# The second product of the last layer by Strassen's scheme, in pairs of column tiles

## The chip, the cores and the metric

One core of a Trainium2 chip runs the whole program in one launch. The metric is the device time of that launch in microseconds (us), from the median of several executions. TensorE (PE) multiplies, VectorE (DVE) and ScalarE (ACT) split operands and evict sums, GpSimd (POOL) helps in some stages, and SyncE's queue (SP) issues most transfers.

## The reference, cut to what matters

Four layers work on x of 2048 x 640: a spectral filter, a token-mixing MLP, and both again. The last layer is the second MLP. S = 2048 tokens, D = 640 channels, F = 1728 hidden units:

```python
def _B_ref(x, w1, b1, w2, b2):
    h = _layernorm(x, axis=-1)                   # (B, S, D)
    u = jnp.einsum("bsd,sf->bdf", h, w1) + b1    # (B, D, F)
    u = _gelu(u)
    y = jnp.einsum("bdf,fs->bds", u, w2) + b2    # (B, D, S)
    return y.transpose(0, 2, 1)
x = x + _B_ref(_layernorm(x, axis=-1), B_w1, B_b1, B_w2, B_b2)
```

All is float32 at the inputs and outputs.

## The kernel before, in words

Each float32 operand is split into two float16 parts, a high one (`wh`, `hh`, `uh`) and a low one (`wl`, `hl`, `ul`); a product is three matmuls, high x high, high x low and low x high (`mm3`). A matmul has 128 rows of contraction, 128 output partitions and 320 of the 640 columns, so a tile of results takes two banks of PSUM, one per half `a`; `big()` gives out such two-bank tiles, four in all.

`b` is the MLP; it is called with `li` = 1 and `li` = 3, and `last` is true for the second. Its first product makes 14 tiles of 128 hidden units (the 14th has 64, held twice), each over 16 tiles of tokens: 16 x 6 matmuls a tile, 64 for the 14th. For the first two tiles PE does the products with the high parts first (`high`) and those with the low parts `hl` of the input behind them (`rest`), since `hl` is made meanwhile on DVE. A tile's sums go through bias and GELU (names `t` and `q`) and are split into `uh[ft]` and `ul[ft]`.

The second product makes 16 column tiles j, each over the 14 tiles of hidden units and two halves: 13 x 2 x 3 matmuls, and 2 x 2 for the last tile, of which one of each two has 64 rows (`wl[:64, ft]`). `wsplit` makes a tile's `wh` on ACT and `wl` on DVE from the raw weights, one tile ahead; `wload` issues the loads on SP's queue three tiles ahead. The bias goes onto the residual `xt` on ACT, and one DVE instruction a tile adds the scaled sums to it, in two halves for the last tile, where PE takes half 0 first. Then `xt` is stored.

A scheduler orders the instructions of each engine where code isn't pinned (`self.pin`); the start of `b` is pinned, the rest of it isn't.

Of the kernel before, what the change touches and what calls it, by code (L numbers as in the profile page):

```python
# [53 lines left out]
class Layers:  # L54
# [41 lines left out]
    def setup(self):  # L96
        nc, A = self.nc, self.A
        base = self.base = self.push("base", side="left")
        self.psum = self.push("ps", bufs=4, space=PSUM)
        self.dram = self.push("dr", space=DRAM)  # L100
        self.mh = base.tile([128, 1], F32, name="mh")
        nc.vector.memset(self.mh, -0.5)
        self.eps = base.tile([128, 1], F32, name="eps")
        nc.vector.memset(self.eps, EPS)
        self.b1 = base.tile([128, NFT], F32, name="b1s")
        self.b2 = base.tile([128, NJ], F32, name="b2s")
        self.junk = base.tile([128, 8, 128], BF16, name="junk")
# [5 lines left out]
        self.qt = base.tile([128, NFT], F32, name="qt")  # L113
        self.su, self.iu = (base.tile([128, 1], F32, name=a) for a in ("su", "iu"))
# [690 lines left out]
    def wtile(self, m):  # L805

        return (0, m, NJ) if m < NFT else (1, m - NFT, NFT)

    def wload(self, m):
        k, t, n = self.wtile(m)  # L810
        src = self.A["w2" if k else "w1"][t]
        raws = self.wraws[m] = []
        for c in (0, n // 2):
            raws.append(self.t(self.wr[max(m - 2, 0) % 3], [128, 8, 128], F32, "raw", 2)[:, :n // 2])
            self.nc.sync.dma_start(raws[-1], src[:, c:c + n // 2])
# [5 lines left out]
    def wsplit(self, m, cs=(0, 1), hi=True, lo=True, part=slice(None)):  # L821

        V, T, (k, t, n) = self.V, self.T, self.wtile(m)
        sc = self.st[k][:, t:t + 1]
        (wh, wl), raws = self.w[m], self.wraws[m]
        for c in cs:
            raw, a = raws[c][:, part], slice(c * n // 2, c * n // 2 + n // 2)
            h, l = wh[:, a][:, part], wl[:, a][:, part]
            if m == NFT - 1:

                T.activation(h[:, :, :64], raw[:, :, :64], AF.Identity, scale=sc)
                T.activation(l[:, :, 64:], raw[:, :, 64:], AF.Identity, scale=sc)
                V.scalar_tensor_tensor(
                    h[:, :, 64:], raw[:, :, 64:], sc, l[:, :, 64:], op0=ALU.mult, op1=ALU.subtract
                )
# [7 lines left out]
    def b(self, li):  # L843
        nc, A = self.nc, self.A
        V, G, T = self.V, self.G, self.T
        mm = self.PE.matmul
        first, last = li == 1, li == 3
        ph = self.push("h", side=self.sq)
# [11 lines left out]
        self.pop("hf")  # L860
        self.wr[1:] = (self.push(a, side=self.sp) for a in ("wr", "wr2"))
# [3 lines left out]
        if first:  # L865
            pf = self.push("uf", side=self.sp)
            uf = [pf.tile([128, 2, 320], F32, name=f"uf{f}_{self.n}") for f in range(NFT)]
            sc = {m: self.scale1(m) for m in range(2, NFT + NJ)}
        p = self.push("b1", side=self.sq)
# [16 lines left out]
        def step(m):  # L886
            if first and m in sc:
                next(sc[m])

        def usplit(ft, t):  # L890
            if first:
                V.tensor_scalar(uh[ft], t, self.su, None, op0=ALU.mult)
            else:
                T.activation(uh[ft], t, AF.Identity, scale=self.su)
            c = slice(0 if ft < NFT - 1 else 64, 128)
# [35 lines left out]
        for j in high(1, pss[1], w[1]):  # L931
            if first and j in (8, 10):
                self.scan1(2, (j // 2 - 4,))
            if j == 15:
                step(2)
        for ft in range(NFT):
# [9 lines left out]
            for j in run:  # L946
# [3 lines left out]
                elif ft == 1:  # L950
                    if j in (1, 2):
                        next(steps)
                    if first and j in (8, 10):
                        self.scan1(3, (j // 2 - 4,))
                    if j == 15:
                        step(3)
                else:
                    if ft == 2 and j in (4, 5):
                        step(3)
                    if first and ft == 2 and j in (5, 6):  # L960
                        self.scan1(4, (j - 5,))
# [4 lines left out]
                    if ft == 2 and j in (10, 11) or ft > 2 and j in (4, 5):  # L966
                        step(ft + 2)
                    if first and j == 8 and ft == NFT - 3:
                        self.scale_u()
                    if first and j in (11, 13):  # L970
# [3 lines left out]
                    if first and ft == NFT - 1 and 6 <= j:  # L974
                        usplit(j - 6, uf[j - 6])
# [14 lines left out]
            T.activation(q, q, AF.Tanh, scale=GS * GC)  # L990
            if first:
                V.scalar_tensor_tensor(uf[ft], q, 1.0, t, op0=ALU.add, op1=ALU.mult)
            else:
                V.scalar_tensor_tensor(t, q, 1.0, t, op0=ALU.add, op1=ALU.mult)
                usplit(ft, t)
        if first:
            for k in range(10, NFT):
                usplit(k, uf[k])
            self.pop("uf")
# [4 lines left out]
        if not last:  # L1004
            self.a0_open()
            for q in range(4):
                self.a0_load_m(q)
            self.a0_load()
        else:
            self.pT = self.push("a0", side=self.sp)  # L1010
        p = self.pT
# [13 lines left out]
        for j in range(NJ):  # L1025
# [10 lines left out]
            order = [(ft, a) for ft in range(NFT) for a in range(2)]  # L1036
            if last and j == NJ - 1:
                order.sort(key=lambda q: q[1])
            for i, (ft, a) in enumerate(order):
                if i in (4, 8):  # L1040
                    next(steps, None)
                if i in (6, 7):
                    step(m + 2)
                if first and i in (15, 18):
                    self.scan1(m + 3, (i // 3 - 5,))
# [8 lines left out]
            x2 = xt.rearrange("p (a b) -> p a b", a=2)  # L1054
            if last and j == NJ - 1:
                for a in range(2):
                    V.scalar_tensor_tensor(x2[:, a], ps[:, a, :320], c2, x2[:, a], op0=ALU.mult, op1=ALU.add)
                    nc.sync.dma_start(self.xs[li + 1][j][:, a * 320:a * 320 + 320], x2[:, a])
                continue
            V.scalar_tensor_tensor(x2, ps[:, :, :320], c2, x2, op0=ALU.mult, op1=ALU.add)  # L1060
            nc.sync.dma_start(self.xs[li + 1][j], xt)
            if last:
                continue
            if j == NJ - 1:
# [11 lines left out]
        self.pop("wb")  # L1076

    def run(self):
        nc, A = self.nc, self.A
        self.setup()  # L1080
        self.wa = self.push("wa", side="left")
        self.wp, self.wr = [self.wa, None], [self.push("wraw", side="left"), None, None]
        self.w, self.wraws = {}, {}
# [242 lines left out]
def _layout(inp):  # L1326
# [7 lines left out]
    a["w1"] = g("B_w1").reshape(128, 16, 1728)[:, :, fi].reshape(128, 16, 14, 128).transpose(2, 0, 1, 3)  # L1334
    a["w2"] = g("B_w2")[fi].reshape(14, 128, 128, 16).transpose(3, 1, 0, 2)
    a["b1"] = g("B_b1")[fi].reshape(14, 128).T
    a["b2"] = g("B_b2").reshape(128, 16)
# [26 lines left out]
```

## Time and profile before

| | us |
|---|---|
| median of 3 runs | 1085.15 (1084.61 to 1086.13) |
| the profiled execution | 1084.86 |
| its span, first to last instruction | 1083.1 |
| last layer, first product, to PE's change of product | 723.4 to 894.05 |
| last layer, second product | 894.05 to 1078.95 |
| last instruction behind PE's end | some 4.1 |

| engine | busy in the span | share |
|---|---|---|
| PE | 1030.8 us | 95% |
| DVE | 643.6 us | 59% |
| ACT | 553.9 us | 51% |
| POOL | 289.4 us | 27% |

The rows are from one profiled execution. Times count from the first instruction. "PE busy" counts a matmul from its start to its modelled end, and since matmuls overlap, the distance between starts is what one costs in a stream.

### The profile page before, as it was taken

The numbers are of one execution on the slowest core, as the hardware profiler recorded it, in microseconds if no ns is written. First come the engines' busy times: TensorE is split into PE (matmuls) and PEld (weight loads), VectorE is DVE, ScalarE is ACT, GpSimd is POOL, SyncE is SP. The second block draws the span as 40 slices with busy tenths as digits, with TensorE's granted clock in tenths as the row PEclk, the third lists the DMA queues.
The fourth block names the chain that finished last, engine by engine and source line by source line (L and its number), as shares of the span: only waits on it lengthen the run. The fifth ranks groups of instructions, "written<-read, shape, count | busy, mean of one in ns | idle before, by whom it ended". The sixth has DMA issues, their size and how long they took to land.

```text
span 1083.1 us, 21299 instructions
## 1 busy us (share of the span) xinstructions
PE 1030.8 (95%) x8515; PEld 777.2 (72%) x8515; DVE 643.6 (59%) x1311; ACT 553.9 (51%) x860; POOL 289.4 (27%) x491
## 2 busy tenths in 40 slices
PE   4889798999999999999997998999999999999998
PEld 3768698777777767777776878877777776666665
DVE  7979879954335856566746995995343334223221
ACT  5857768675445555555432775864433344222220
POOL 6938877200000002211221886840000000000000
PEclk8599999999999999999998998999999999999999
DMA  7766255523222264444224633644222233433411
GB/s 234 255 192 193 80 195 184 185 89 104 82 79 68 69 240 134 138 126 130 84 76 129 207 97 130 212 146 156 83 91 81 81 106 113 161 118 133 158 51 37
DMA packets 55738, 141.48 MB, mean 131 GB/s; under 512 B 6460, under 2 KB 12248, under 8 KB 55384
## 3 DMA queue, kind: packets, MB, share of 16 engines
q1 hardware_dynamic: 54200, 131.97, 37.5%
q0 software_dynamic: 1440, 8.15, 2.4%
q8 instruction: 67, 1.10, 0.4%
q14 instruction: 31, 0.25, 0.1%
HBM read 117.03 MB, written 23.07 MB: 129 GB/s over the span
## 4 chain that ended last, share of the span: by engine, by line
PE 76%; DVE 16%; POOL 2%; issue 2%; ACT 1%; DMA 1%; SPq 0%; DVEq 0%; ACTq 0%; POOLq 0%
PE ps L46 76%; DVE xt L46 5%; DVE st L46 2%; DVE el L46 2%; DVE f L46 2%; DVE s1l L46 1%; DVE hl L46 1%; DVE ta L46 1%; DVE xl L46 1%; DMA xt<-x 1%; POOL eo L46 0%; POOL ta L46 0%; DMA rest<-s1l 0%; DVE tb L46 0%; DVE mv L46 0%
## 5 line engine op out<-in xcount | busy, mean ns | idle before, releaser
L46 PEld LDWEIGHTS <-wh 128*128 128x128 f16 x3520 | 340.0, 98 | 138.3 <-issue 1.8
L46 PE MATMUL ps<-uh,wl 128*128 128x320 f16 (+1 forms) x896 | 268.4, 300 | 0.0
L46 PE MATMUL ps<-ul,wh 128*128 128x320 f16 x896 | 267.3, 299 | 0.0
L46 PE MATMUL ps<-uh,wh 128*128 128x320 f16 x832 | 248.9, 299 | 0.0
L46 PEld LDWEIGHTS <-wl 128*128 128x128 f16 x1728 | 168.7, 98 | 76.6 <-issue 8.7
L46 DVE SCALAR_TENSOR_TENSOR wl<-raw,s,wh 128x896 f16<-128x896 f32 (+2 forms) x120 | 139.2, 1173 | 112.9 <-ACT wh L46 112.6
L46 PE MATMUL ps<-hh,wh 128*128 128x320 f16 x896 | 194.8, 299 | 1.4 <-ACT hh L46 1.4
L46 ACT ACTIVATE wh<-raw,s 128x896 f16<-128x896 f32 (+2 forms) x124 | 126.6, 1044 | 131.0 <-PE ps L46 130.3
L46 PE MATMUL ps<-hl,wh 128*128 128x320 f16 x896 | 184.8, 299 | 0.0
L46 PE MATMUL ps<-hh,wl 128*128 128x320 f16 x832 | 181.1, 299 | 0.0
L46 POOL TENSOR_TENSOR r<-v,mh 128x1 f32<-128x1 f32 x64 | 35.8, 559 | 340.8 <-DVE nm L46 325.3
L46 DVE SCALAR_TENSOR_TENSOR xt<-ps,c,xt 128x640 f32<-128x640 f32 (+1 forms) x33 | 28.4, 863 | 139.6 <-PE ps L46 135.9
L46 ACT ACTIVATE junk<-raw 128x896 bf16<-128x896 f32 (+1 forms) x60 | 59.6, 993 | 48.5 <-DMA raw<-w 48.3
L46 ACT ACTIVATE xt<-xt,b2s 128x640 f32<-128x640 f32 x32 | 26.3, 821 | 91.1 <-DMA xt<-x 90.9
L46 DVE TENSOR_TENSOR f<-eo 128x256 f32<-128x256 f32 (+1 forms) x128 | 40.1, 366 | 41.8 <-POOL eo L46 41.2
L46 PE MATMUL ps<-tDi,yh 128*128 128x322 f32 x256 | 61.1, 326 | 2.6 <-ACT yh L46 1.7
L46 DVE BATCH_NORM_STATS2 st<-xt 128x6 f32<-128x320 f32 x128 | 56.2, 481 | 5.1 <-DMA xt<-x 4.9
L46 POOL TENSOR_TENSOR eo<-z 128x320 f32<-128x320 f32 x63 | 54.2, 881 | 17.0 <-ACT z L46 15.1
L46 PE MATMUL ps<-ph,tS 128*128 128x321 f16 (+2 forms) x288 | 57.9, 286 | 0.0
L46 PE MATMUL ps<-tM,f 128*128 128x128 f32 x160 | 38.3, 409 | 20.4 <-DMA xt<-x 11.9
L46 ACT ACTIVATE z<-xt,nb,r 128x640 f32<-128x640 f32 x31 | 28.5, 919 | 54.1 <-POOL z L46 43.6
L46 PEld LDWEIGHTS ps<-tM,f 128*128 128x128 f32 x160 | 32.3, 290 | 26.2 <-DVE f L46 25.7
(142 smaller groups left out, 1678.9 us busy)
## 6 DMA issues: line engine op xcount, KB each, us to landing
raw<-w SPq DMA_DIRECT2D x56, 512.0 KB
raw<-w SPq DMA_DIRECT2D x64, 448.0 KB
xt<-x SPq DMA_DIRECT2D x80, 320.0 KB
w<-w SPq DMA_DIRECT2D x48, 321.0 KB
x<-xt SPq DMA_DIRECT2D x48, 320.0 KB
out<-xt SPq DMA_DIRECT2D x15, 320.0 KB
tIM<-tIM POOLq DMA_DIRECT2D x8, 512.0 KB, 4.7
tDi<-tDi POOLq DMA_DIRECT2D x2, 1932.0 KB, 9.9
```

What stands on the lines that cost most here:

```text
L46: i = f(*a, **k)
```

## The change

The last layer has its own function now, `b2nd`; `b1st` is the old `b` without its branches for the last layer. In `b2nd` the second product takes column tiles d and d + 8 together, d = 0 to 7. The 14 tiles of hidden units are seen as seven in an upper half and seven in a lower half; the two halves of columns are 320 each. So a pair is a product of 2 x 2 quarters, A11, A12, A21, A22 of the weights by B11, B12, B21, B22 of the hidden units. Strassen's scheme (Winograd's form) makes it from seven products of quarters: A11 B11, S1 T1, S2 T2, S3 T3, A12 B21, S4 B22, A22 T4. The S are sums and differences of weight quarters (128 x 896, formed on DVE by `form`), the T are differences of quarters of the hidden units (`usums`, on DVE in the first product). Each product is seven tiles of contraction by one `mm3`, 21 matmuls of 128 rows. The lower half's 14th tile is filled with zeros in a copy of the weights (`w2z`).

The first product takes its tiles in the order `SEQ`: 6, 13, then 0, 7, 1, 8 and so on, so that tiles t and t + 7 stand together and tile 13, the one with 64 units, is the second. The hidden units are kept as seven quarters per t, high and low.

In the second product the loop over n = 0 to 55 is pinned on all engines. At step n PE gets product n, then the eviction of product n - 1 is issued, the high split of product n + 3 (ACT), the low split of n + 2 (DVE), and the forming of an operand four or five products ahead. Products 0 to 3 are arranged so that products 2 and 3 leave out the tile that was made last (`LATE`) and take it at the end. A11 and S1 of a pair lie in one two-bank tile, S2 and S3 in another, A12 takes the bank of A11, S4 and A22 take the banks of S2 and S3. A product is added to as many quarters of the result as need it. Weights are loaded four tiles ahead. The scale `US` is halved.

```diff
+NQ = 8
+SEQ = [6, 13] + [t + 7 * i for t in range(6) for i in range(2)]
...
     def wtile(self, m):
-        return (0, m, NJ) if m < NFT else (1, m - NFT, NFT)
+        k, i = m // NFT, m % NFT if m < NFT else m - NFT
+        if self.second:
+            i = i // 2 + i % 2 * NQ if k else SEQ[i]
+        return min(k, 1), i, NFT if k else NJ
...
+        u = [pu.tile([128, 2, 7, 320], F16, name=f"u{f}_{self.n}") for f in range(7)]
...
+        PQ = ("A11", "B11"), ("S1", "T1"), ("S2", "T2"), ("S3", "T3"), ("A12", "B21"), ("S4", "B22"), ("A22", "T4")
...
+        def form(n):
...
+            x, y, op = {
+                "S1": ((d, "A21"), (d, "A22"), ADD), "S2": (n - 1, (d, "A11"), SUB),
+                "S3": ((d, "A11"), (d, "A21"), SUB), "S4": ((d, "A12"), n - 3, SUB),
+            }[a]
+            x, y = (src[q] if isinstance(q, int) else raw(*q) for q in (x, y))
+            V.tensor_tensor(s, x, y, op=op)
...
+        def high(m, ps, w):
+            for j in range(NJ):
+                prod(ps, w[0], j, self.h[j][0], start=j == 0)
+                if not dup(m):
+                    prod(ps, w[1], j, self.h[j][0])
...
+        BK = {"A11": (0, 0), "S1": (0, 1), "S2": (1, 0), "S3": (1, 1), "A12": (0, 0), "S4": (1, 0), "A22": (1, 1)}
...
+        def evict(n):
...
+            if a == "A11":
+                part["m1"] = self.t(p, [128, 320], F32, "m1", 2)
+                T.activation(part["m1"], ps, AF.Identity, scale=c)
+                add(x[:, 0, 0], x[:, 0, 0])
+            if a == "S1":
+                add(x[:, :, 1], x[:, :, 1], both2(ps))
+            if a == "S2":
+                part["u2"] = self.t(p, [128, 320], F32, "u2", 2)
+                add(part["u2"], part["m1"])
+                V.tensor_tensor(x[:, 0, 1], x[:, 0, 1], part["u2"], op=ADD)
+            if a == "S3":
+                u3 = self.t(p, [128, 320], F32, "u3", 2)
+                add(u3, part["u2"])
+                V.tensor_tensor(x[:, 1], x[:, 1], both2(u3), op=ADD)
...
+            if a == "A12":
+                add(x[:, 0, 0], x[:, 0, 0])
+            if a == "S4":
+                add(x[:, 0, 1], x[:, 0, 1])
+                nc.sync.dma_start(out[d], row(d, 0))
+            if a == "A22":
+                add(x[:, 1, 0], x[:, 1, 0])
...
+        FORM = {3: 5, 5: 4, 6: 4, 1: 4}
+        for n in range(NP + 1):
+            d, i = n // 7, n % 7
+            if i == 0 and n < NP:
+                bank[d] = self.big(), self.big()
...
+            late = n in (2, 3)
+            if n < NP:
+                js = [j for j in range(7) if j != LATE]
+                product(n, js if late else js + [LATE], not late)
+            if n == 3:
+                for k in (2, 3):
+                    product(k, [LATE])
+            for k in {0: (), 3: (), 4: (2, 3)}.get(n, (n - 1,)):
+                evict(k)
+            if n:
+                hi(n + 3)
+            if n > 1:
+                lo(n + 2)
+            if i in FORM:
+                form(n + FORM[i])
```

At the start of the last layer DVE has, before the change, the last statistic `nb`, the two low splits of the second weight tile, and the low halves `hl`:

```order
L46 TENSOR_SCALAR nm_10281<-mv_10277 128x1
L46 TENSOR_TENSOR nb_10285<-nm_10281,r_10283 128x1
L46 SCALAR_TENSOR_TENSOR wl_9597<-raw_9592,s_72,wh_9596 128x1024
L46 SCALAR_TENSOR_TENSOR wl_9597<-raw_9594,s_72,wh_9596 128x1024
L46 TENSOR_TENSOR hl_1492_10312<-hf_1275_9372,hh_1118_7816 128x640
L46 TENSOR_TENSOR hl_1492_10314<-hf_1275_9373,hh_1118_7817 128x640
```

And DVE at the same place after the change:

```order
L48 TENSOR_SCALAR nm_10285<-mv_10281 128x1
L48 TENSOR_TENSOR nb_10289<-nm_10285,r_10287 128x1
L48 SCALAR_TENSOR_TENSOR wh_9598<-raw_9594,s_72,wl_9599 128x8x64
L48 SCALAR_TENSOR_TENSOR wh_9598<-raw_9596,s_72,wl_9599 128x8x64
L48 TENSOR_TENSOR hl_1492_10316<-hf_1275_9374,hh_1118_7818 128x640
L48 TENSOR_TENSOR hl_1492_10318<-hf_1275_9375,hh_1118_7819 128x640
```

The two splits ahead of `hl` have half as many elements, since the second tile is now the one with 64 units.

In the second product DVE has, before the change, one eviction into `xt` and two splits `wl` per column tile; here are two tiles:

```order
L46 SCALAR_TENSOR_TENSOR xt_11988<-ps_12001,c_75,xt_11988 128x640
L46 SCALAR_TENSOR_TENSOR wl_12095<-raw_11894,s_73,wh_12094 128x896
L46 SCALAR_TENSOR_TENSOR wl_12095<-raw_11896,s_73,wh_12094 128x896
L46 SCALAR_TENSOR_TENSOR xt_11990<-ps_12099,c_75,xt_11990 128x640
L46 SCALAR_TENSOR_TENSOR wl_12193<-raw_11992,s_73,wh_12192 128x896
L46 SCALAR_TENSOR_TENSOR wl_12193<-raw_11994,s_73,wh_12192 128x896
```

After the change DVE has this from the eviction of A11 of a pair to the split of its A22 (`S` are formed operands, `u_` the partial sums u2 and u3, `wh`, `wl`, `wo` places of split operands, `ps_12466` the tile of A11 and S1, `ps_12467` that of S2 and S3):

```order
L48 SCALAR_TENSOR_TENSOR xt_12288<-ps_12466,cp,xt_12288 128x320
L48 SCALAR_TENSOR_TENSOR wh_12491<-S_1647_12464,sp,wh_12491 128x896
L48 TENSOR_TENSOR S_1654_12524<-raw_12167,S_1643_12432 128x896
L48 SCALAR_TENSOR_TENSOR xt_12288<-ps_12466,cp,xt_12288 128x2x320
L48 SCALAR_TENSOR_TENSOR wl_12521<-raw_12167,sp,wl_12521 128x896
L48 SCALAR_TENSOR_TENSOR u_1656_12572<-ps_12467,cp,m_1652_12518 128x320
L48 TENSOR_TENSOR xt_12288<-xt_12288,u_1656_12572 128x320
L48 SCALAR_TENSOR_TENSOR wh_12548<-S_1654_12524,sp,wh_12548 128x896
L48 TENSOR_TENSOR S_1658_12578<-raw_12434,raw_12436 128x896
L48 SCALAR_TENSOR_TENSOR u_1661_12605<-ps_12467,cp,u_1656_12572 128x320
L48 TENSOR_TENSOR xt_12288<-xt_12288,u_1661_12605 128x640
L48 SCALAR_TENSOR_TENSOR wl_12575<-raw_12230,sp,wl_12575 128x896
```

Per pair DVE has 20 instructions there instead of six for two column tiles, and sums of operands and evictions of single products stand between the splits.

## Rows read from the trace of the kernel before

**Rows 1.** The chain that ended last, in order of time: start, us, what.

```profile
723.37 355.66 PE ps L46 x2568
1079.05 0.55 DVE xt L46
```

**Rows 2.** Busy us by stretch, the last layer; last columns: clock, DMA share.

```profile
core 0: us, PE busy (x) PEld busy (x) DVE busy (x) ACT busy (x) POOL busy (x), PEclk, DMA share, GB/s
894.00:1079.00 185.00, 185.00 (x1314) 126.77 (x1312) 50.10 (x50) 45.70 (x50) 0.00 (x0) 1.00 0.33 110
723.40:894.00 170.60, 170.60 (x1256) 122.83 (x1256) 75.75 (x82) 69.75 (x83) 0.00 (x0) 1.00 0.31 102
```

**Rows 3.** Timeline of PE in the last layer: start us, us, engine, line, operation.

```profile
893.78 0.43 PE L46 MATMUL ps<-hl,wh 128*128 128x320 f16 x2
894.05 0.30 PE L46 MATMUL ps<-uh,wh 128*128 128x320 f16 x1
...
1044.28 0.31 PE L46 MATMUL ps<-uh,wh 128*128 128x320 f16 x1
...
1054.88 0.30 PE L46 MATMUL ps<-ul,wh 128*128 128x320 f16 x1
1055.11 0.31 PE L46 MATMUL ps<-uh,wl 64*128 64x320 f16 x1
...
1055.83 0.31 PE L46 MATMUL ps<-uh,wh 128*128 128x320 f16 x1
```

**Rows 4.** Timeline of DVE and PE at the start of the last layer.

```profile
721.50 2.48 DVE L46 SCALAR_TENSOR_TENSOR wl<-raw,s,wh 128x1024 f16<-128x1024 f32 x2
723.88 11.85 DVE L46 TENSOR_TENSOR hl<-hf,hh 128x640 f16<-128x640 f32 x16
733.23 8.86 PE L46 MATMUL ps<-hl,wh 128*128 128x320 f16 x64
741.92 0.43 PE L46 MATMUL ps<-hh,wh 128*128 128x320 f16 x2
```

**Rows 5.** Groups of DVE by form, last layer: busy us, mean ns, idle before.

```profile
L46 DVE SCALAR_TENSOR_TENSOR wl<-raw,s,wh 128x896 f16<-128x896 f32 x32 | 35.5, 1149 | 7.5 <-ACT wh L46 7.3
L46 DVE SCALAR_TENSOR_TENSOR xt<-ps,c,xt 128x640 f32<-128x640 f32 x15 | 13.3, 884 | 120.2 <-PE ps L46 120.2
L46 DVE TENSOR_TENSOR hl<-hf,hh 128x640 f16<-128x640 f32 x16 | 11.8, 823 | 0.0
L46 DVE SCALAR_TENSOR_TENSOR ul<-t,su,uh 128x640 f16<-128x640 f32 x13 | 11.5, 884 | 9.2 <-ACT uh L46 9.2
L46 DVE SCALAR_TENSOR_TENSOR wh<-raw,s,wl 128x512 f16<-128x512 f32 x2 | 1.5, 745 | 0.0
L46 DVE SCALAR_TENSOR_TENSOR xt<-ps,c,xt 128x320 f32<-128x320 f32 x2 | 1.0, 548 | 10.7 <-PE ps L46 10.7
```

**Rows 6.** Busy us by stretch, the wait for `hl` in the first MLP.

```profile
212.00:217.00 5.00, 4.16 (x32) 2.81 (x31) 4.82 (x8) 1.15 (x2) 0.00 (x0) 1.00 0.68 247
```

**Rows 7.** DVE additions of two SBUF operands before the MLPs: group, and one instruction.

```profile
L46 DVE TENSOR_TENSOR xt<-xt,ec 128x320 f32<-128x320 f32 x16 | 15.5, 967 | 0.0
...
717.61 0.48 DVE L46 TENSOR_TENSOR xt<-xt,ec 128x320 f32<-128x320 f32 x1
```

**Rows 8.** Timeline of the second product, and busy us of its last stores.

```profile
929.70 2.21 DVE L46 SCALAR_TENSOR_TENSOR wl<-raw,s,wh 128x896 f16<-128x896 f32 x2
...
1072.93 0.31 PE L46 MATMUL ps<-uh,wl 64*128 64x320 f16 x1
...
1078.71 0.31 PE L46 MATMUL ps<-uh,wl 64*128 64x320 f16 x1
1079.05 1.01 DVE L46 SCALAR_TENSOR_TENSOR xt<-ps,c,xt 128x320 f32<-128x320 f32 x2 [10.68 <-PE ps L46]
...
1080.50:1081.50 1.00, 0.00 (x0) 0.00 (x0) 0.00 (x0) 0.00 (x0) 0.00 (x0) 1.00 0.92 324
```

**Rows 9.** ACT: group of weight splits by form, and one eviction of 322.

```profile
L46 ACT ACTIVATE wh<-raw,s 128x896 f16<-128x896 f32 x32 | 31.7, 1035 | 38.1 <-PE ps L46 38.1
714.05 0.43 ACT L46 ACTIVATE ec<-ps 128x322 f32<-128x322 f32 x1
```

More of the change, by code (lines that the diff above doesn't have):

```diff
@@ L113, in setup @@
         self.qt = base.tile([128, NFT], F32, name="qt")
+        self.s2, self.c2 = (base.tile([128, NQ], F32, name=f"{a}p") for a in "sc")
+        self.second, self.nr = False, 3
         self.su, self.iu = (base.tile([128, 1], F32, name=a) for a in ("su", "iu"))
@@ L828, in wsplit @@
             h, l = wh[:, a][:, part], wl[:, a][:, part]
[L829 to L835, printed above, removed]
+            if (k, t) == (0, NFT - 1):
+                if hi:
+                    T.activation(h[:, :, :64], raw[:, :, :64], AF.Identity, scale=sc)
+                    T.activation(l[:, :, 64:], raw[:, :, 64:], AF.Identity, scale=sc)
+                if lo:
+                    V.scalar_tensor_tensor(
+                        h[:, :, 64:], raw[:, :, 64:], sc, l[:, :, 64:], op0=ALU.mult, op1=ALU.subtract
+                    )
                 continue
@@ L846, in b @@
         mm = self.PE.matmul
-        first, last = li == 1, li == 3
         ph = self.push("h", side=self.sq)
@@ L860, in b @@
         self.pop("hf")
-        self.wr[1:] = (self.push(a, side=self.sp) for a in ("wr", "wr2"))
+        self.wr[1:3] = (self.push(a, side=self.sp) for a in ("wr", "wr2"))
         pu = self.push("u", side=self.sp)
@@ L864, in b @@
         ul = [pu.tile([128, 2, 320], F16, name=f"ul{f}_{self.n}") for f in range(NFT)]
[L865 to L868, printed above, removed]
+        pf = self.push("uf", side=self.sp)
+        uf = [pf.tile([128, 2, 320], F32, name=f"uf{f}_{self.n}") for f in range(NFT)]
+        sc = {m: self.scale1(m) for m in range(2, NFT + NJ)}
         p = self.push("b1", side=self.sq)
@@ L886, in step @@
         def step(m):
-            if first and m in sc:
+            if m in sc:
                 next(sc[m])
         def usplit(ft, t):
[L891 to L894, printed above, removed]
+            V.tensor_scalar(uh[ft], t, self.su, None, op0=ALU.mult)
             c = slice(0 if ft < NFT - 1 else 64, 128)
@@ L931, in b @@
         for j in high(1, pss[1], w[1]):
-            if first and j in (8, 10):
+            if j in (8, 10):
                 self.scan1(2, (j // 2 - 4,))
@@ L952, in b @@
                         next(steps)
-                    if first and j in (8, 10):
+                    if j in (8, 10):
                         self.scan1(3, (j // 2 - 4,))
@@ L959, in b @@
                         step(3)
-                    if first and ft == 2 and j in (5, 6):
+                    if ft == 2 and j in (5, 6):
                         self.scan1(4, (j - 5,))
@@ L967, in b @@
                         step(ft + 2)
-                    if first and j == 8 and ft == NFT - 3:
+                    if j == 8 and ft == NFT - 3:
                         self.scale_u()
-                    if first and j in (11, 13):
+                    if j in (11, 13):
                         self.scan1(ft + 3, (j // 2 - 5,))
@@ L973, in b @@
                         step(ft + 3)
-                    if first and ft == NFT - 1 and 6 <= j:
+                    if ft == NFT - 1 and 6 <= j:
                         usplit(j - 6, uf[j - 6])
@@ L990, in b @@
             T.activation(q, q, AF.Tanh, scale=GS * GC)
[L991 to L999, printed above, removed]
+            V.scalar_tensor_tensor(uf[ft], q, 1.0, t, op0=ALU.add, op1=ALU.mult)
+        for k in range(10, NFT):
+            usplit(k, uf[k])
+        self.pop("uf")
         self.pop("b1")
@@ L1003, in b @@
         self.sp, self.sq = self.sq, self.sp
[L1004 to L1010, printed above, removed]
+        self.a0_open()
+        for q in range(4):
+            self.a0_load_m(q)
+        self.a0_load()
         p = self.pT
@@ L1036, in b @@
             order = [(ft, a) for ft in range(NFT) for a in range(2)]
-            if last and j == NJ - 1:
-                order.sort(key=lambda q: q[1])
             for i, (ft, a) in enumerate(order):
@@ L1043, in b @@
                     step(m + 2)
-                if first and i in (15, 18):
+                if i in (15, 18):
                     self.scan1(m + 3, (i // 3 - 5,))
@@ L1054, in b @@
             x2 = xt.rearrange("p (a b) -> p a b", a=2)
[L1055 to L1059, printed above, removed]
             V.scalar_tensor_tensor(x2, ps[:, :, :320], c2, x2, op0=ALU.mult, op1=ALU.add)
             nc.sync.dma_start(self.xs[li + 1][j], xt)
-            if last:
-                continue
             if j == NJ - 1:
@@ L1081, in run @@
         self.wa = self.push("wa", side="left")
-        self.wp, self.wr = [self.wa, None], [self.push("wraw", side="left"), None, None]
+        self.wp, self.wr = [self.wa, None], [self.push("wraw", side="left"), None, None, None]
         self.w, self.wraws = {}, {}
@@ L1150, in run @@
         for i in range(2):
+            self.second = i == 1
             self.a1(i == 0)
             self.a2(2 * i)
-            self.b(2 * i + 1)
+            (self.b2nd if i else self.b1st)(2 * i + 1)
+            self.wr[1:] = [None] * 3
         for k in reversed(list(self.open)):
```

220 lines of the change are left out of this document (216 added, 4 removed).

## The prediction

> **What bounds the kernel now.** I read the chain of waits first: it ends in one unbroken piece of TensorE work, from 723.37 to the end of the second product of the last layer [rows 1]. The busy time by stretch then says what stands beside it. In both halves of the last layer PE is busy in every microsecond at granted clock 1.00 (the 2.4 GHz level), DVE is busy for 75.75 us of 170.6 and for 50.10 of 185.0, POOL for nothing, DMA for a third [rows 2]. So the stretch is worth exactly its matmul slots, and DVE and ACT have room. The matmul starts show the slots: from 741.92 to 894.05 lie the first product's 1,120 matmuls, 0.1358 us each [rows 3, 4]. In the second product one column tile takes from 1044.28 to 1055.83, 11.55 us, and all sixteen from 894.05 to 1078.95, 184.9 us. Its 82 matmuls at 0.1358 would take 11.14. The other 0.42 sits around the two matmuls with 64 rows: their starts and those behind them are 0.23 to 0.24 apart [rows 3].
>
> **The matmuls removed and added.** Sixteen tiles x 82 = 1,312 matmuls become 56 products x 7 tiles x 3 = 1,176, all with 128 rows (the half-empty tile is padded with zeros). At 0.1358 that is 159.7 us for 184.9: **25.2 us less**, 18.5 by count and 6.7 from the gaps. The gaps are at the 64-row form and not at the end of a sum: at 894.05 a sum ends and the next begins, and the starts stay on their step [rows 3]. The Trainium skill says otherwise: "TensorE: Matmul & The Clock Gate", section "Why this matters for your kernels", gives a matmul of few rows the time of a full one. By it the change would save 18.5 and the time would be near 1069; the rows of this kernel differ, 0.24 against 0.136.
>
> **The start of the first product.** The new order of tiles puts the half-filled tile second. Its high part is 32 matmuls where the old second tile had 64, so PE comes 32 x 0.1358 = 4.35 us sooner to the matmuls that need the low halves hl of the input. Before, PE reached them at 733.23, DVE finished the sixteenth at 735.73, and PE needed it at 737.3: 1.6 us of slack [rows 4]. DVE gains too: two splits of 1024 elements (2.48 us) become two of 512, 0.745 each [rows 4, 5], 1.33 on DVE's step. So hl begins at 722.83 and ends at 722.83 + 11.85 = 734.68; PE runs its last pair behind it and leaves that tile near 735.1, where 4.35 us sooner would be 733.22. **+1.9 us**, bounds 1.6 to 2.3 (DVE's step against its full durations). The same total of matmuls is left. The first layer has the same wait, and the clock stays at 1.00 in it [rows 6], so I add nothing for the clock. ScalarE has four half splits instead of two whole ones in the stage before, at most 0.6 us; it idles there between tiles, so 0, bound 0.6.
>
> **The rest of the first product.** DVE adds per two tiles four differences and splits seven quarters instead of four, some 5 us in 26 us where it is half idle [rows 2]; ACT likewise. PE waits there for weight splits alone, which stand ahead of these in both engines' order. Cost 0: the cover is the idle half. Loads move one tile earlier (four in flight); the DMA engines are busy a third of the time, 0.
>
> **The steady second product.** Per pair of column tiles PE has 147 slots, 19.96 us. DVE has 7 splits at 1.149, 6 evictions of 320 at 0.548, one of 640 at 0.884, one addition of 640 at 0.823 and one of 320 at 0.48 [rows 5, 7]; the four operand sums of 896 are in no row: from 0.48 at 320 and 0.823 at 640 I estimate 1.10. Sum 17.9 us by durations. Back to back the instructions overlap: two splits take 2.21, not 2.30, and sixteen hl 11.85, not 13.2 [rows 4, 8], so each costs some 0.085 less: 16.2 us. Either way under 19.96. ACT has 7 splits at 1.035 and three smaller ones [rows 9], under half.
>
> But the order has one narrow place. The eviction of half a two-bank tile waits for all matmuls of that tile: in the last tile the first half's sum was complete at 1072.93, and both evictions started at 1079.05, 0.34 after the last matmul started [rows 8]. A11 and S1 share such a tile, so A11's eviction waits for the end of S1. From there DVE does, in order: eviction of A11, split of S3, sum S4, eviction of S1, split of A12, the two steps of S2's eviction, split of S4, sum S1 of the next pair, first step of S3's eviction. Only then may PE write S4 into the tile of S2 and S3. PE gets there three products later, 63 x 0.1358 = 8.56 us. DVE by its step: 0.20 + 0.46 + 1.06 + 1.01 + 0.80 + 1.06 + 0.55 + 0.40 + 1.06 + 1.01 + 0.55 = 8.16. Slack 0.4, less a hand-over that no row isolates. By full durations it is 8.85, and PE waits 0.3 to 0.4 in each of 8 pairs. So **0 to 3.1 us**; I take 0, since the rows of two splits and of sixteen hl are the nearest and both show the overlap. All other hand-overs have 0.8 us or more: a split for product n + 2 is done during product n.
>
> **The change of product.** The last tile's activations run in halves. From half-width durations of 0.43 (ACT) and 0.55 (DVE) [rows 5, 9] and two splits of 640 at 0.884 I estimate its last operand 7.2 us after the first product ends. Products 0 to 3 leave 78 slots, 10.6 us, before any of T2, T3 of that tile is needed: covered. Behind it on DVE stand A11's eviction, S4's sum, S1's eviction and A12's split, done at 10.6; PE needs that at 11.4. S4's tile is free at 14.1 against 14.26. Bounds 0 to 0.8, I take **+0.2**. Input rows and weights are loaded before that; SP's queue waits for buffers there that are read two products or more earlier.
>
> **The tail.** Evictions of 320 twice behind the last matmul, as now. But the last stores are 320 and 160 KB where both were 160. 320 KB took one microsecond at 324 GB/s [rows 8]: **+0.4**, bounds 0 to 0.6.
>
> **The sum.** -25.2 + 1.9 + 0 + 0.2 + 0.4 = -22.7. The profiled execution took 1084.86 (span 1083.1 and 1.76 outside), so 1062.2; the median lies 0.3 above that execution: **1062.5 us**. Ends: -25.2 + 1.6 = -23.6 gives 1061.6; all upper bounds, -25.2 + 2.3 + 0.6 + 3.1 + 0.8 + 0.6 = -17.8, give 1067.4.
>
> **Rivals.**
> - DVE pays full durations at the narrow place, as worked out: +3.1, **1065.6**. For it: the evictions that depend on each other cannot overlap, and I have no row of four kinds alternating. Against: the pairs of splits [rows 8]. The Trainium skill's "VectorE: DVE Perf Modes", section "The DRAIN you can't avoid", says that the next operation starts only when the pipe is empty, which would be this case; the 2.21 for two of 1.149 differs from it. Chance 0.18.
> - The gaps belong to ends of sums, not to 64-row matmuls: then 6.7 us are not all won and 56 ends cost up to 0.1 each: 1062.5 + 5.6 = **1068**. Against: the step at 894.05. Chance 0.04.
> - Slower than before: DVE becomes the bound. Operations with two SBUF inputs took 0.967 in the stage before instead of 0.48 [rows 7]. If the 13 such ones of a pair (13.7 us) doubled, DVE had 31.6 us per pair and the time were 1062.5 + 8 x 11.6 = **1155**. It decides from 19.96 + 22.7/8 = 22.8 us per pair, 27% above my 17.9. Against: POOL ran additions beside them there and does nothing in the last layer [rows 2]. Chance 0.03.
> - The change does not do what it says, since operands come late in every pair and PE gives the slots back: needs 2.8 us of waiting per pair, and no split is that late. Time near **1085**, chance 0.01.
>
> **How the numbers follow.** The forecast has 0.74. The range 1060.8 to 1067.4 takes in it and the first rival, with 0.8 us below the lowest sum for the spread of runs. This kernel's times can tell about 0.2% (2.2 us) from no change. Faster 0.96, same 0.01, slower 0.03.
>
> **What would show it.** Right: 1,176 matmuls behind the change of product with starts 0.136 apart and no row with 64 rows; PE waits for hl of 1 to 2 us in sum near 735, with the stage behind it 1.9 us late; DVE busy 16 to 18 us per pair; POOL still at 0. Wrong: PE idle before the first matmul of each S4 with DVE u3 as the releaser (first rival), gaps at every 21st matmul (second), DVE busy throughout (third), or the granted clock under 1.00 in either product, of which nothing is in the sum.

## The result, and the profile after

| | before | after |
|---|---|---|
| median, us | 1084.88 (1084.06 to 1086.13, 4 runs) | 1068.47 (1067.23 to 1069.54, 4 runs) |
| ratio | | 0.9847 (95% interval 0.983 to 0.9864) |
| the profiled execution, its span | 1084.86, 1083.1 | 1067.23, 1065.3 |
| wait for the last `hh` to PE's change of product | 723.37 to 894.05: 170.68 | 722.01 to 894.07: 172.06 |
| second product | 894.05 to 1078.95: 184.9 | 894.07 to 1060.72: 166.65 |
| end of PE to end of span | 4.15 | 4.6 |

The change wins 16.4 us. The forecast was 1062.5, its range ended at 1067.4, so the kernel is 6.0 us slower than forecast and 1.1 above the range. The three stretches of the table give the difference: +1.4, -18.25 and +0.45 are -16.4. The two spans differ by 17.8, because PE's wait for the last `hh` also ended 1.4 earlier in the profiled execution of the kernel after. That stage, ahead of the last layer, ended between 719.8 and 726.1 us in the profiled executions of this study, so lengths of stretches are compared below, not where they stand in a trace. (The end of PE is put one step behind the start of its last matmul: 0.14, and 0.24 before, where that one has 64 rows. Spans are given to 0.1 us, so the stretch behind it is good to 0.1.)

Busy time by stretch, the kernel after, to be read against [rows 2]. Columns: length, busy us of PE, weight loads, DVE, ACT, POOL, granted clock, DMA share, GB/s.

```profile
722.00:894.00 172.00, 171.22 (x1256) 122.80 (x1256) 101.19 (x127) 79.61 (x96) 0.00 (x0) 1.00 0.33 108
894.00:1060.70 166.70, 160.91 (x1178) 114.89 (x1176) 129.58 (x161) 72.14 (x85) 0.00 (x0) 1.00 0.36 114
```

PE has its 1,176 matmuls and the clock is at 1.00 (2.4 GHz), but PE is no longer busy throughout: 5.8 us of the second product are idle, where [rows 2] show none. DVE's busy time went from 50.10 to 129.58 us, still under the length of the stretch. The chain of waits of the kernel after says where the idle time lies. Columns: start, us, what ("issue" is time in which the engine waits for nothing that the profile shows).

```profile
930.20 17.29 PE ps L48 x126
947.51 0.56 DVE u L48
948.13 0.37 issue
948.50 1.15 DVE wh L48
949.65 1.00 DVE S L48
950.65 0.47 DVE u L48
951.17 17.29 PE ps L48 x126
```

In [rows 1] one piece of PE work ran to the end. Now it is cut into pieces of 126 matmuls, six products of 21 from S4 of one pair to S3 of the next, and between two pieces stands DVE work from u2 to u3. The pieces begin 20.97 us apart; 147 matmuls at 0.1358 are 19.96. The timeline of PE, the kernel after, shows the place (a product is one row of x21 or a third of one of x63; in brackets the idle time and its releaser):

```profile
944.46 3.02 PE L48 MATMUL ps<-u,wh 128*128 128x320 f16 x21
947.31 3.02 PE L48 MATMUL ps<-u,wl 128*128 128x320 f16 x21
951.17 3.01 PE L48 MATMUL ps<-u,wh 128*128 128x320 f16 x21 [0.84 <-DVE u L48]
954.02 3.02 PE L48 MATMUL ps<-u,wl 128*128 128x320 f16 x21
```

The rows are S3, A12, S4 and A22 of pair 2. Starts are 2.85 apart, 21 x 0.1358, except at S4: 3.86, so 1.01 us are lost (the bracket says 0.84 because a matmul's modelled end lies behind the next one's earliest start). The releaser is DVE's `u`. DVE at the same place, the kernel after:

```profile
942.37 0.55 DVE L48 SCALAR_TENSOR_TENSOR xt<-ps,cp,xt 128x320 f32<-128x320 f32 x1 [2.13 <-ACT m L48]
...
945.69 1.14 DVE L48 SCALAR_TENSOR_TENSOR wl<-raw,sp,wl 128x896 f16<-128x896 f32 x1
947.51 0.55 DVE L48 SCALAR_TENSOR_TENSOR u<-ps,cp,m 128x320 f32<-128x320 f32 x1 [0.68 <-PE ps L48]
948.10 0.49 DVE L48 TENSOR_TENSOR xt<-xt,u 128x320 f32<-128x320 f32 x1
948.50 1.15 DVE L48 SCALAR_TENSOR_TENSOR wh<-S,sp,wh 128x896 f16<-128x896 f32 x1
949.57 1.08 DVE L48 TENSOR_TENSOR S<-raw,raw 128x896 f32<-128x896 f32 x1
950.57 0.54 DVE L48 SCALAR_TENSOR_TENSOR u<-ps,cp,u 128x320 f32<-128x320 f32 x1
```

DVE is early, not late: it idles 0.68 us for PE before u2, the first step of S2's eviction. S2's last matmul stands just ahead of the start of S3, 944.46. But u2 starts at 947.51, 0.2 behind the start of A12, and thus behind the end of **S3**. S2 and S3 lie in one two-bank tile. From there DVE does u2, an addition, the split of S4, a sum and u3, which PE needs before S4: from 947.31 to 951.17 are 3.86 us, and PE's own work in them, A12, is 2.85.

Pair 0 has a stall too, with another cause. PE, the kernel after, A12 and S4 of pair 0:

```profile
905.48 3.02 PE L48 MATMUL ps<-u,wl 128*128 128x320 f16 x21
909.23 3.01 PE L48 MATMUL ps<-u,wh 128*128 128x320 f16 x21 [0.73 <-DVE u L48]
```

These starts are 3.75 apart where 2.85 would do, so 0.90 are lost. The place on ACT and DVE where this begins, one view of each, the kernel after:

```profile
900.27 1.53 ACT L48 ACTIVATE xt<-xt,b2s 128x640 f32<-128x640 f32 x2
901.72 0.51 ACT L48 ACTIVATE m<-ps,cp 128x320 f32<-128x320 f32 x1
```

```profile
902.26 0.55 DVE L48 SCALAR_TENSOR_TENSOR xt<-ps,cp,xt 128x320 f32<-128x320 f32 x1 [0.88 <-ACT m L48]
```

DVE could have evicted A11 at 901.4, but it waits for ACT's copy `m` of the same bank, which is queued behind the biases of both rows of `xt`; from there on DVE works without a pause to u3.

### The profile page after: what moved, and what is told of

It is laid out like the page before. It is cut to its first block, busy times and chain, and to the rows that moved or that the text cites. A ratio compares the mean times of both kernels' runs of the same rounds, so it can differ in the third digit from the quotient of the medians.

```text
span 1065.3 us, 21213 instructions
## 1 busy us (share of the span) xinstructions
PE 1007.0 (95%) x8379; PEld 765.4 (72%) x8379; DVE 747.9 (70%) x1468; ACT 590.3 (55%) x910; POOL 289.3 (27%) x491
## 4 chain that ended last, share of the span: by engine, by line
PE 72%; DVE 20%; issue 2%; POOL 2%; ACT 2%; DMA 1%; SPq 0%; POOLq 0%; DVEq 0%; ACTq 0%
PE ps L48 72%; DVE xt L48 5%; DVE st L48 3%; DVE hl L48 2%; DVE el L48 2%; DVE f L48 2%; DVE s1l L48 1%; DVE wh L48 1%; DVE S L48 1%; DVE u L48 1%; DVE ta L48 1%; DVE xl L48 1%; DMA xt<-x 1%; POOL eo L48 1%; POOL ta L48 0%
## 5 line engine op out<-in xcount | busy, mean ns | idle before, releaser
L48 PEld LDWEIGHTS <-wh 128*128 128x128 f16 x2992 | 289.6, 98 | 123.8 <-issue 10.3
L48 PEld LDWEIGHTS <-wl 128*128 128x128 f16 (+1 forms) x1616 | 157.7, 98 | 67.0 <-issue 4.2
L48 DVE SCALAR_TENSOR_TENSOR wl<-raw,s,wh 128x1024 f16<-128x1024 f32 (+2 forms) x88 | 103.7, 1182 | 95.3 <-ACT wh L48 93.5
L48 ACT ACTIVATE wh<-raw,s 128x1024 f16<-128x1024 f32 (+2 forms) x92 | 94.9, 1048 | 75.4 <-PE ps L48 69.6
L48 PE MATMUL ps<-uh,wl 128*128 128x320 f16 x448 | 134.2, 300 | 0.0
L48 PE MATMUL ps<-ul,wh 128*128 128x320 f16 x448 | 133.6, 299 | 0.0
L48 PE MATMUL ps<-uh,wh 128*128 128x320 f16 x416 | 124.3, 299 | 0.0
L48 PE MATMUL ps<-u,wo 128*128 128x320 f16 x504 | 69.9, 299 | 0.0
L48 PEld LDWEIGHTS <-wo 128*128 128x128 f16 x504 | 49.3, 98 | 19.1
L48 PE MATMUL ps<-u,wh 128*128 128x320 f16 x336 | 48.4, 299 | 5.8 <-DVE u L48 5.8
```

The lines of the kernel that those rows point to most:

```text
L48: i = f(*a, **k)
```

## Experiments

The lengths below are from the trace of each kernel, in us, and the last column has the median of its times: from PE's wait for the last `hh` to the change of product; the second product; a pair (starts of S4 in pairs 3 and 4); from PE's end to the span's end.

| kernel | first product | second product | pair | end | median, runs |
|---|---|---|---|---|---|
| before | 170.68 | 184.9 | | 4.15 | 1084.88, 4 |
| after | 172.06 | 166.65 | 20.97 | 4.6 | 1068.47, 4 |
| after, again | 172.06 | 166.6 | 20.97 | 4.6 | 1068.42, 4 |
| e1, products apart | 172.06 | 160.63 | 19.97 | 3.65 | 1062.13, 4 |
| e2, S2 and S3 together | 172.06 | 166.64 | 20.97 | 3.66 | 1067.01, 4 |
| e3, order | 172.06 | 162.04 | 20.20 | 4.6 | 1064.65, 4 |
| e4, twice | 172.06 | 179.56 | 22.10 | 4.55 | 1085.68, 10 |
| e5, apart and twice | 172.06 | 161.74 | 19.97 | 3.7 | 1062.27, 1 |
| e6, 128 rows, on before | 170.68 | 178.22 | | 4.2 | 1073.17, 4 |
| e7, half tile fourth | 171.99 | 166.63 | 20.97 | 4.6 | 1068.14, 4 |
| e8, half tile eighth | 170.69 | 166.62 | 20.97 | 4.6 | 1067.62, 5 |
| e9, order and A11 first | 172.06 | 159.73 | 19.97 | 4.55 | 1061.29, 4 |
| e10, best | 170.69 | 159.73 | 19.97 | 3.75 | 1058.49, 4 |

**e1: neighbours in different tiles.**

```diff
+        BN = {"A11": (0, 0), "S1": (1, 0), "S2": (0, 1), "S3": (1, 1), "A12": (0, 0), "S4": (1, 0), "A22": (0, 1)}
+        at = lambda n: (BN if ops[n][0] else BK)[ops[n][1]]
-        place = lambda n: bank[ops[n][0]][BK[ops[n][1]][0]][:, BK[ops[n][1]][1], :320]
+        place = lambda n: bank[ops[n][0]][at(n)[0]][:, at(n)[1], :320]
```

> The changed kernel with other banks from pair 1 on: A11, S2, A12 and A22 in one two-bank tile, S1, S3 and S4 in the other, so that no two products in a row share a tile. Theory T (S2's eviction waits for the end of S3, since both lie in one tile): PE's stall of 1.01 us before S4 goes in pairs 1 to 6, a pair takes 19.96 us instead of 20.97, 6.1 us less; the end is some 0.5 to 0.9 shorter, because S4's last eviction and store no longer wait for A22. Median 1061.0 to 1062.0 for 1068.5. Theory D (DVE's durations at the narrow place that was forecast, from A11's eviction on): A11's eviction starts 2.85 us earlier, and the stall goes too. Theory B (DVE or PE bound by its own work, not by a wait): a pair stays at 20.97 and the median within 1 us of 1068.

Measured 1062.13 (1061.01 to 1062.76), ratio to before 0.9788 (0.9774 to 0.9803). Every stall of pairs 1 to 6 is gone; of PE's waits in the second product one is left, 0.7 us for DVE's `u` in pair 0, whose banks are as they were. DVE, e1, u2 and u3 of pair 2:

```profile
944.50 0.55 DVE L48 SCALAR_TENSOR_TENSOR u<-ps,cp,m 128x320 f32<-128x320 f32 x1 [0.68 <-PE ps L48]
...
947.56 0.55 DVE L48 SCALAR_TENSOR_TENSOR u<-ps,cp,u 128x320 f32<-128x320 f32 x1
```

In e1 S3 began at 944.30, so u2 now follows the end of S2 by 0.2, one product sooner than before, and u3 is done 1.9 us before S4's start at 950.01. That excludes theory B. It doesn't decide between T and D, which both expected it, since A11 and S1 were parted too.

**e2: only S2 and S3 share a tile.**

```diff
+        BN = {"A11": (0, 0), "S1": (1, 0), "S2": (0, 1), "S3": (0, 0), "A12": (1, 1), "S4": (0, 1), "A22": (1, 0)}
```

(used from pair 1 on, as in e1)

> The changed kernel with A11 apart from S1 and S4 apart from A22, but S2 and S3 still in one tile (A11, S2, S3, S4 in the first tile of a pair, S1, A12, A22 in the second), from pair 1 on. Theory T (sharing by S2 and S3 is the cause): a pair stays at 20.97 us and DVE still waits for PE before S2's eviction; only the end is 0.5 to 0.9 shorter, median 1067.6 to 1068.0. Theory D (the chain on DVE from the end of S1 is too long, as the rival on record had it): A11's eviction starts 2.85 us earlier, the chain has that much slack, a pair takes 19.96, median 1061.0 to 1062.0.

Measured 1067.01 (1065.81 to 1068.01): the pair stays at 20.97, to the hundredth. DVE, e2:

```profile
970.30 0.55 DVE L48 SCALAR_TENSOR_TENSOR u<-ps,cp,m 128x320 f32<-128x320 f32 x1 [3.53 <-PE ps L48]
```

DVE has everything from A11's eviction to A12's split done 3.53 us early, and then waits for the end of S3 as before. This decides between T and D: a DVE that stands idle for 3.53 us is not too slow. Only the end is shorter, 3.66 us for 4.6: S4's eviction no longer waits for A22, and its store of 320 KB leaves one product sooner.

**e3: the same DVE work in another order.**

```diff
-            for k in {0: (), 3: (), 4: (2, 3)}.get(n, (n - 1,)):
-                evict(k)
+            if i != 3:
+                for k in () if not n else (n - 2, n - 1) if i == 4 else (n - 1,):
+                    evict(k)
```

> The changed kernel with its banks, but S2's eviction moved on DVE behind the split of S4 and the forming of the next S1, next to S3's eviction (as pair 0 has it already). Nothing is removed. Theory T: the split and the sum run while DVE would wait for the end of S3; from there to the last read by u3 are 0.2 + 0.59 + 0.41 + 0.55, 1.75 us against 2.85 of PE's A12, so the stall goes: 19.96 per pair, median 1062.0 to 1062.8. Theory D: the same DVE work lies between the end of S1 and u3, so the stall of 1.0 stays, median 1068 to 1069.

Measured 1064.65 (1063.54 to 1066.41), 2 us above what T said. The pair fell to 20.20, not 19.96. DVE, e3, pair 3 (S1 ended at 964.85):

```profile
965.61 0.55 DVE L48 SCALAR_TENSOR_TENSOR xt<-ps,cp,xt 128x320 f32<-128x320 f32 x1 [2.13 <-ACT m L48]
966.07 1.14 DVE L48 SCALAR_TENSOR_TENSOR wh<-S,sp,wh 128x896 f16<-128x896 f32 x1
...
972.05 0.55 DVE L48 SCALAR_TENSOR_TENSOR u<-ps,cp,m 128x320 f32<-128x320 f32 x1
972.63 0.49 DVE L48 TENSOR_TENSOR xt<-xt,u 128x320 f32<-128x320 f32 x1
973.04 0.55 DVE L48 SCALAR_TENSOR_TENSOR u<-ps,cp,u 128x320 f32<-128x320 f32 x1
```

Now DVE does not wait before u2, and from A11's eviction to u3 one instruction follows the next. With the wait for S3 covered, the next limit appears, and it is the "narrow place" of the forecast: from the end of S1 to the end of u3 8.7 us, for PE's 8.56. The first row shows what the forecast's 8.16 lacked: DVE's eviction of A11 waits for ACT's `m`, some 0.55 us longer than it would for PE.

**e9: DVE's eviction of A11 ahead of ScalarE's copy, on e3.**

```diff
                 part["m1"] = self.t(p, [128, 320], F32, "m1", 2)
+                add(x[:, 0, 0], x[:, 0, 0])
                 T.activation(part["m1"], ps, AF.Identity, scale=c)
-                add(x[:, 0, 0], x[:, 0, 0])
```

> The kernel with S2's eviction moved (e3), and besides DVE's eviction of A11 ahead of ScalarE's copy m1 of the same bank, where it waited for that copy (0.54 us). In e3 DVE's chain from the end of S1 (964.87) to the end of u3 (973.59) took 8.72 us and PE's three products 8.56, a stall of 0.24 per pair by the starts. Theory N (this is the narrow place that was forecast, 8.16 by DVE's steps, plus the wait for m1): the chain falls to 8.2, the stall goes, 19.97 per pair for 20.20, 1.4 us less than e3 in pairs 1 to 6, median 1063.0 to 1063.5. Rival: the chain is set by something else on the way, pairs stay at 20.20, median 1064.6.

Measured 1061.29 (1060.35 to 1064.12), 1.7 under the lowest that was expected. Pair 0 gained as well, 0.9 us by the trace; the rest is less than the spread of its runs. DVE, e9:

```profile
963.52 0.55 DVE L48 SCALAR_TENSOR_TENSOR xt<-ps,cp,xt 128x320 f32<-128x320 f32 x1 [1.57 <-PE ps L48]
...
970.95 0.54 DVE L48 SCALAR_TENSOR_TENSOR u<-ps,cp,u 128x320 f32<-128x320 f32 x1
```

S1 ended at 963.32; u3 ended at 971.49, 8.17 us later, and the pair is 19.97. So the durations and steps of the forecast were right to a few hundredths, and the rival of full durations (8.85) is excluded. That an eviction on DVE waits for ACT's read of the same bank is what the trace of the kernel after shows in all eight pairs; the Trainium skill, "PSUM — Partial Sum Buffer", section "PSUM bank collisions raise a hardware error", says that two engines may not access one bank, in the same partitions, at the same time, reads included. The program's order follows it. The rule speaks of banks; the wait of u2 for S3 is between two banks of one tile, and e1 shows that it is not needed when the tile is another.

**e4: one more DVE instruction per pair at that place.**

```diff
+            if i == 3:
+                form(n + FORM[i])
```

> The changed kernel with one more DVE instruction per pair (the sum S1 of the next pair is formed twice) between S2's and S3's evictions, in pairs 0 to 6. DVE is busy for 15.6 us of a pair before it. Theory T: each costs its full 1.0 us on PE's path: a pair takes 21.97, +7.0 us, median 1075.0 to 1076.0. Theory B (the pair is bound by something else than this stretch of DVE): 0 to 1 us, median 1068 to 1069.5.

Measured 1085.68 (1081.02 to 1086.63), 10 us more than even T expected: the whole gain of the change is gone. PE, e4, S4 of pairs 3 and 4, and the granted clock around S4 of pairs 3, 4 and 5 (PE alone):

```profile
980.77 3.01 PE L48 MATMUL ps<-u,wh 128*128 128x320 f16 x21 [1.97 <-DVE u L48]
...
1002.87 4.69 PE L48 MATMUL ps<-u,wh 128*128 128x320 f16 x21 [1.97 <-DVE u L48]
```

```profile
980.00:985.00 5.00, 4.23 (x32) 1.00 0.25 67
1002.50:1007.50 5.00, 4.63 (x22) 0.66 0.28 89
1026.50:1031.50 5.00, 4.86 (x24) 0.66 0.28 92
```

The instruction itself costs 1.13 per pair on PE's path, where T said 1.0: 22.10 for 20.97. The rest is the clock. In pairs 4, 5 and 6 the product behind the stall takes 4.52 us for 2.85, with a granted clock of 0.66 in the 5 us around it, a mean of the two levels of 1.2 and 2.4 GHz; in pairs 1 to 3 the same stall leaves it at 1.00. 7 x 1.13 + 3 x 1.67 = 12.9 is the difference of the second products (179.56 and 166.65). The median lies 17.2 above the kernel after, more than the 12.9. In the two profiled executions the difference is 16.8, of which 4.1 lie ahead of the last layer, where the code is the same; how often the clock falls in the other executions one trace can't tell.

**e5: the same instruction where the products are apart** (the edits of e1 and e4 together).

> The kernel with the products apart (e1) and the same additional DVE instruction per pair between the evictions of S2 and S3 as in e4. There u3 ended at 948.11 for a product S4 that began at 950.01, so 1.9 us are free at that place, and DVE waits for some 3 us per pair elsewhere. Theory T: the 1.1 us of the additional instruction fit into the 1.9, pairs 1 to 6 stay at 19.97 us, only pair 0 (whose banks are unchanged) is 1.1 longer; 1062.0 to 1064.0. Theory B (DVE's work as such sets the time, and the additional instruction costs wherever it stands): 1.1 per pair or more, 1069 and above.

Measured 1062.27 in one run. Pairs 1 to 6 stay at 19.97, only pair 0 is 1.1 longer (161.74 for 160.63). The same instruction costs 1.13 us a pair in e4 and nothing here: DVE's amount of work is not what PE waits for.

**e6: the 64-row matmuls of the kernel before with 128 rows.**

```diff
-                    mm(o, wl[:64, ft], uh[ft][:64, a], start=False, stop=True)
+                    mm(o, wl[:, ft], uh[ft][:, a], start=False, stop=True)
```

> The kernel before, with 128 rows in the 32 matmuls of the second product that have 64 (the half-filled tile's low x high product also takes the tile's other 64 rows, which changes the result). The count of matmuls stays at 1,312. Theory R (the rows of before: starts at the 64-row matmuls are 0.23 to 0.24 apart, others 0.1358): a column tile takes 82 x 0.1358 = 11.14 us instead of 11.55, the second product 178.2 for 184.9, median 1078.2 to 1079.0. Theory S (the Trainium skill, TensorE: Matmul & The Clock Gate, section Why this matters for your kernels: a matmul of few rows takes the time of a full one, so nothing is to be won by filling it): 0, median 1085.

Measured 1073.17 (1072.29 to 1074.68), 12.0 less than before, twice what theory R said. The expectation overlooked that `b` is both MLPs: the first one's second product is 6.6 us shorter by the trace too (189.3 for 195.9, from its first matmul's start to its last's). In the last layer it is 178.22 for 184.9, as R has it. The two are 13.3 together, of which the medians show 12.0; where the rest went is not shown. The change and e10 leave the 64-row matmuls of the first MLP as they are, so that gain is still open. Matmuls of PE in the same 100 us, e6:

```profile
900.00:1000.00 100.00, 100.00 (x739) 1.00 0.43 143
```

and the kernel before:

```profile
900.00:1000.00 100.00, 100.00 (x711) 1.00 0.39 134
```

Both are busy throughout at clock 1.00, yet one gets 28 more matmuls through. So a 64-row matmul among 128-row ones costs more than a full one here, and 6.7 us of the change's gain came from filling rows. Theory S, by which there is nothing to win, doesn't hold for this stream. PE's busy time doesn't show such a loss; only the spacing of starts does [rows 3].

**e7 and e8: the half-filled tile fourth, and eighth.**

```diff
-SEQ = [6, 13] + [t + 7 * i for t in range(6) for i in range(2)]
+SEQ = [t + 7 * i for t in (0, 1, 2, 6, 3, 4, 5) for i in range(2)]
...
-                prod(ps, w[0], j, self.h[j][1])
-                prod(ps, w[1], j, self.h[j][0], stop=j == NJ - 1)
+                prod(ps, w[0], j, self.h[j][1], stop=dup(m) and j == NJ - 1)
+                if not dup(m):
+                    prod(ps, w[1], j, self.h[j][0], stop=j == NJ - 1)
```

(e8; e7 has 0, 6, 1, 2, 3, 4, 5 in the first line)

> The changed kernel with the order 0, 7, 6, 13, then 1, 8 and so on for the tiles of the first product, so that the tile with 64 units comes fourth and not second; banks and the second product as changed. Theory H (PE comes to the products with the low halves hl too early, because the second tile has 32 matmuls fewer in its high part): PE's waits for hl of 0.77 us in sum near 732 go, and from the first wait for hh to the change of product PE takes 170.7 us as before instead of 172.1: 1.4 us less, median 1066.7 to 1067.4. Rival: the fourth tile gives ACT and DVE half the time for its neighbours' splits and evictions, PE waits there instead, 0 or slower.

> The changed kernel with the tile of 64 units eighth in the first product (order 0, 7, 1, 8, 2, 9, 6, 13, 3, ...), the second product as changed. In e7, with that tile fourth, PE's waits for hl were gone, but ScalarE's queue stood for 15.1 us behind the load of its weights, and PE waited 0.35 and 0.60 us for the third tile's splits. Theory H (the short high part of the second tile is what costs the 1.4 us, and e7 lost them again at that load): neither wait is left, from the wait for hh to the change of product 170.7 us for 172.1, median 1066.7 to 1067.4. Rival: the half-empty tile costs about the same wherever it stands, 172 us, median 1068.4.

PE at the start of the last layer, the kernel after, to be read against [rows 4]:

```profile
727.52 3.49 PE L48 MATMUL ps<-hl,wh 128*128 128x320 f16 x24
731.31 0.43 PE L48 MATMUL ps<-hl,wh 128*128 128x320 f16 x2 [0.30 <-DVE hl L48]
732.05 0.57 PE L48 MATMUL ps<-hl,wh 128*128 128x320 f16 x3 [0.30 <-DVE hl L48]
732.78 4.97 PE L48 MATMUL ps<-hl,wh 128*128 128x320 f16 x35 [0.17 <-DVE hl L48]
737.59 0.43 PE L48 MATMUL ps<-hh,wh 128*128 128x320 f16 x2
```

The 64 matmuls take 10.07 us from 727.52 to 737.59, where 64 x 0.1358 are 8.69: 1.38 lost. e7 measured 1068.14 (1067.5 to 1068.57), no gain. Its waits for `hl` are gone, and two others came, PE in e7:

```profile
742.27 0.45 PE L48 MATMUL ps<-hh,wh 128*128 128x320 f16 x2 [0.35 <-ACT wh L48]
743.59 0.45 PE L48 MATMUL ps<-hh,wl 128*128 128x320 f16 x2 [0.60 <-DVE wl L48]
```

The waits of ACT in e7, summed from 720 to 760 (us, times, longest):

```profile
ACT wl L48 <- DMA raw<-w: 15.1, 1, 15.1
```

ACT waits for the load of the fourth tile's weights, and the third tile's splits stand behind that in ACT's order. With the tile eighth (e8) no wait is left: PE works in one piece of 1,256 matmuls, 170.69 us, 1.37 less than after. By medians e8 is 1067.62 (1066.55 to 1069.53), 0.8 less, which is under what the times alone can tell; the trace decides. Theory H holds, and e7's rival had a part of the truth.

**e10: e1, e8 and the swap of e9 together.**

> Three edits together: products in a row in different two-bank tiles (e1), DVE's eviction of A11 ahead of ScalarE's copy (as in e9), the tile of 64 units eighth (e8). If the terms are what they were found to be apart: second product 159.7 us with no wait (166.7 as changed), start 1.4 less, end 0.5 to 0.9 less: 8.9 to 9.3 us under the changed kernel, 1059.2 to 1059.6, and 25.3 to 26.0 under the kernel before. If the terms overlap, or another place becomes late: 1060.5 and above.

Measured 1058.49 (1057.32 to 1060.1), ratio to before 0.9759 (0.9745 to 0.9772): 26 us under the kernel before and 10 under the change. The chain of waits of e10 ends as [rows 1] did, in one piece (this view leaves out steps of about 1 us and less):

```profile
718.49 1.10 POOL xt L48
724.13 330.60 PE ps L48 x2432
```

The terms add up by the traces: 1.37 at the start, 6.92 in the second product and 0.85 at the end are 9.1 us, of the 9.9 between the medians. The kernel after, run again beside it, had 1068.42 (1067.08 to 1068.85):

> The changed kernel itself once more, beside the two others on the same chip. 1067.2 to 1069.5, as before; the stage up to the last layer varies by some us from run to run, so that in its trace only the lengths of stretches are compared: a pair 20.97 us, first matmul of the second product to the end of the last 166.7.

## Why the forecast was off, step by step

- **The matmuls, -25.2: right.** e10 shows it bare: 159.73 us for 184.9, at the forecast's 0.1358 a matmul. The two parts are right by themselves, too: e6 takes the 6.7 us of the 64-row matmuls alone (184.9 to 178.22), and the other 18.5 are the count. The rival that put the gaps at the ends of sums falls with it: 56 sums end in e10, and none of these ends shows a gap.
- **The start, +1.9 (1.6 to 2.3): the mechanism right, the size 1.38.** The forecast let PE wait for the sixteenth `hl` before it began with the second tile's low products. In the program's order four matmuls of the second tile stand ahead of the last pair of the first, and they fill 0.54 us of the wait.
- **The rest of the first product, 0: right.** No wait of PE between 737.59 and 894.07, with DVE busy for 101.19 us where [rows 2] have 75.75.
- **The steady second product, 0 (0 to 3.1): the step that failed.** It cost 6.0 us, 1.0 in each of pairs 1 to 6 (20.97 for 19.97; pair 7 has no next pair to form). The forecast stated the rule itself, that an eviction waits for all matmuls of its two-bank tile, and applied it to A11 and S1. For S2, which shares a tile with S3, it counted the eviction as two DVE steps in a row of others, with no wait of its own, and let "all other hand-overs" have 0.8 us or more. With the rule applied, its own steps give 0.20 + 0.55 + 0.40 + 1.06 + 1.01 + 0.55 = 3.77 from the end of S3, for the 2.85 of A12, so 0.9 per pair. e2 shows the cause alone, e3 and e1 two ways out.
- **The narrow place, 8.16 against 8.56: right as a sum, short by one wait.** With the 0.55 us for ACT's copy it is 8.7 (e3), without it 8.17 (e9). It was hidden behind the wait for S3.
- **The change of product, +0.2 (0 to 0.8): 0.90.** The forecast let A11's eviction follow the last operand. It waited 0.88 us longer, for ACT's copy, which stood behind two bias instructions on ACT, and that came out as the 0.90 that PE lost at S4 of pair 0. In e9, without the wait, pair 0 has no stall. So the same missing wait, an eviction's wait for ACT's read of its bank, stands behind this term and the one before.
- **The end, +0.4: right** (4.6 for 4.15).
- **The first rival** named the right sign, PE idle before S4 with u3 as releaser, and a wrong cause: DVE's steps overlap as the rows of before showed (the split at 948.50 lasts 1.15, the next instruction begins 1.07 later). The paragraph of the Trainium skill that the forecast cites for it ("VectorE: DVE Perf Modes", section "The DRAIN you can't avoid") also says that a next operation that is not held starts earlier, so the Trainium skill is not against these rows. The slower rival, DVE as the bound, has e5 against it: 1.1 us more work a pair cost nothing.

With the two missed waits, 6.0 and 0.7 more than forecast, less 0.5 at the start, the forecast of 1062.5 would have been 1068.7.

## What to carry to other kernels

When buffers are handed over at the grain of a tile, list for every read the last write into the same tile that stands ahead of it in the program, and start the chain there; apply a rule found in the trace to every pair that it fits, not to the first. Products that follow each other belong in different tiles, so that an eviction can begin while the next product runs: that alone was worth 6 us of 1068 here. Before sizing a chain by durations, write down for each instruction on it what else than the instruction before releases it, other engines' reads of the same bank among them.

## What the runs showed of the hardware

Two things were not expected. In e4's trace stalls of 1.97 us came once in 22 us. Those of pairs 1 to 3 left the clock at 1.00; each of pairs 4 to 6 was followed by a product that took 1.67 us longer, at a mean clock of 0.66 in the 5 us around it. Stalls of 0.84 never did that (kernel after, e2). And a matmul with 64 rows among ones with 128 costs more than a full one: filling the rows of 32 of them shortened a product by 6.7 us with the same count of instructions (e6).
